# Who issues the loads of the weight ring: POOL or SP

## The chip, the cores and the metric

The kernel runs on one core of a Trainium2 chip. A core has a matrix engine (TensorE, PE in the profile; PEld is its weight load), a vector engine (VectorE, DVE), an engine for activations and copies (ScalarE, ACT), a general one (GpSimd, POOL) and one that mostly issues DMAs (SyncE, SP). Each has its own instruction queue and takes it in order. The metric is the device time of one execution in microseconds, as the median of several runs. Lower is better.

## The reference

Eight batches of sliding-window attention with a distance bias, then a maxout layer:

```python
scores = scale * np.matmul(q, k.transpose(0, 1, 3, 2))        # q, k, v: 8 x 8 heads x 576 x 64
mask = (rel >= 0) & (rel < 128)
scores = np.where(mask, scores + bias[None], -1000000000.0)
...                                                           # softmax over keys
attn_out = np.matmul(attn, v)
x = attn_out.transpose(0, 2, 1, 3).reshape(B * S, H * D)      # 4608 x 512
h = np.maximum(np.maximum(x @ w1, x @ w2), x @ w3)            # w1, w2, w3: 512 x 768
return h @ w_out                                              # w_out: 768 x 512
```

## The kernel before

Attention works on pairs of heads: four tasks per batch, five blocks of 128 queries each. `load` (line 288) and `load_v` (line 293) fetch the inputs of a task through SP into pools of two buffers. `products` (314), `score` (344, 348), `normalise` (367), `turn` (transposes, 376, and mask cuts on POOL, 390 and 394) and `mix` (416) compute it.

The maxout layer of a batch is a sequence of 11 groups: nine of the three weight matrices, cut into columns (`g` below 9), and two of the output matrix (`g` 9 and 10 of the unit's count, which read the resident tiles `ow`). From batch 1 on each group multiplies 2 x 2 blocks with seven products in place of eight, so a group has seven units, a batch 77, and a unit is 6 matmuls (9 for the output matrix) of 128 x 128 by 128 x 288 at line 623. Every operand is held as a high and a low part, and each product takes three matmuls. `factors_x` and `factors_h` build the sums and differences of the blocks; `split` (442 on ACT, 443 on POOL or DVE) makes the high and low parts. `put` takes results out of PSUM: maxima and sums on DVE (544 to 552), copies on ACT (632), and at line 537 the store of an output tile through SP.

The seven factor tiles of a group's weights are computed once, in the first two batches, and kept in DRAM as `keep[g][a]`, in two halves: `a` 0 with four tiles (1024 KB) and `a` 1 with three (768 KB). From batch 2 on they are read back for each batch. This is the weight ring: the pool `wt_p` has `RING = 2` buffers for each half. `stream` is called at the end of each unit and puts the next load into the program, if `ahead` says that the last unit that reads the buffer two groups back has been written down:

```python
def ahead(n, a):
    return (n - RING, 6 if a else 3) in used
```

The units of a group come in the order 0, 1, 6 of the group before, 2, 3, 4, 5. Units 0 to 3 read half 0; units 4, 5 and 6 read half 1. So half 1 comes free two units before half 0 of the next group does, and the loads come in pairs.

All events of the program are sorted by a due time written by hand (`at`), and a tile framework then orders each engine's queue at compile time, places the waits, and lets an instruction that needs a buffer wait until the buffer's last reader is through. From batch 2 on, `pe` keeps the matmuls in the order of the program (`tc.keep_in_program_order`, 277); the other engines' orders are the framework's.

After the last batch's attention (from about 721 us) the rest is the maxout layer alone: this document calls it the tail.

Of the kernel before, what the change touches and what calls it, by code (L numbers as in the profile page):

```python
# [8 lines left out]
F32 = mybir.dt.float32  # L9
# [20 lines left out]
def attention_maxout_kernel(  # L30
# [11 lines left out]
    nc = tc.nc  # L42
# [76 lines left out]
    keep = [[dram.tile([P, e, 2, W], F32, name=f"keep{g}_{a}") for a, e in enumerate((4, 3))] for g in range(9)]  # L119
# [3 lines left out]
    wts = {}  # L123
# [87 lines left out]
    def place(n, a):  # L211
        wts[n, a] = wt_p.tile([P, 4 - a, 2, W], F32R, name=f"wt{a}")

    def ahead(n, a):

        return (n - RING, 6 if a else 3) in used
# [48 lines left out]
    def stream():  # L265
        nonlocal streamed
        n, a = divmod(streamed, 2)
        if n < 9 * B and prepared == STEPS and ahead(n, a):
            place(n, a)
            nc.gpsimd.dma_start(wts[n, a], keep[n % 9][a])  # L270
            streamed += 1

    fixed = False
# [319 lines left out]
    def unit(u):  # L593
# [33 lines left out]
        if g < 9:  # L627
            used.add((at, k))
        stream()
        if k < 3:  # L630
            e = part_of[n, "e", k] = t_p.tile([P, C], F32, name="t")
# [112 lines left out]
```

## Time and profile before

| | |
|---|---|
| median of 3 runs | 817.06 us (815.86 to 818.38) |
| the profiled execution | 818.97 us |
| its span, first to last instruction | 817.3 us |
| mean granted clock of TensorE | 0.970 |
| bytes moved by DMA | 187.96 MB, of which 99.10 MB by the loads that POOL issues |
| busy share of PE, PEld, DVE, ACT, POOL | 93%, 82%, 66%, 65%, 34% |

In a line of a timeline or of the chain, the first number is the start in us from the start of the span and the second the length in us; a bracket at the end gives the idle time of the engine before the instruction and what ended it. A line of waits has the total in us, the number of times and the longest. A line of DMA issues has the count, the size of one in KB and the median time from issue to landing. A line of windows has the stretch, its length, the busy time of PE, PEld, DVE, ACT and POOL with their instruction counts, the granted clock, the busy share of the 16 DMA engines and GB/s. "SPq" and "POOLq" are the queues of the engines that issue DMAs.

### The profile page before, as it was taken

The numbers are of one execution on the slowest core, as the hardware profiler recorded it, in microseconds if no ns is written. First come the engines' busy times: TensorE is split into PE (matmuls) and PEld (weight loads), VectorE is DVE, ScalarE is ACT, GpSimd is POOL, SyncE is SP. The second block draws the span as 40 slices with busy tenths as digits, with TensorE's granted clock in tenths as the row PEclk, the third lists the DMA queues.
The fourth block names the chain that finished last, engine by engine and source line by source line (L and its number), as shares of the span: only waits on it lengthen the run. The fifth ranks groups of instructions, "written<-read, shape, count | busy, mean of one in ns | idle before, by whom it ended". The sixth has DMA issues, their size and how long they took to land.

```text
span 817.3 us, 18140 instructions
## 1 busy us (share of the span) xinstructions
PE 761.5 (93%) x6344; PEld 673.1 (82%) x6344; DVE 538.2 (66%) x1756; ACT 528.7 (65%) x1736; POOL 281.8 (34%) x515
## 2 busy tenths in 40 slices
PE   4767998999889999999999999999999999999987
PEld 1335988898778898899888998899888998899887
DVE  5777878479997756693757756694657746573552
ACT  6988888478776656676667656676667656552332
POOL 1211223111433325542544325542544325531431
PEclk7776999999999999999999999999999999999999
DMA  7875786388888458863887458873787457855851
GB/s 268 279 243 171 246 280 214 111 287 272 289 278 299 138 190 292 285 238 135 263 279 257 165 192 293 281 241 133 268 272 258 163 192 264 253 181 186 303 179 59
DMA packets 53772, 187.96 MB, mean 230 GB/s; under 512 B 5936, under 2 KB 14896, under 8 KB 46768
## 3 DMA queue, kind: packets, MB, share of 16 engines
q0 software_dynamic: 15552, 99.10, 36.6%
q1 hardware_dynamic: 37984, 87.64, 31.5%
q8 instruction: 50, 0.82, 0.4%
q14 instruction: 42, 0.34, 0.1%
q10 hardware_dynamic: 144, 0.07, 0.0%
HBM read 154.53 MB, written 32.24 MB: 229 GB/s over the span
## 4 chain that ended last, share of the span: by engine, by line
PE 61%; DVE 9%; issue 9%; DMA 8%; POOL 6%; ACT 6%; SPq 0%; POOLq 0%; DVEq 0%; ACTq 0%
PE ps_m L623 41%; PE ps_x L416 6%; PE ps_m L585 6%; PE ps_s L314 5%; POOL hs L443 4%; PE pt L376 4%; DMA hs<-w 2%; DMA wt<-keep 2%; DMA hs<-in_w_all 2%; ACT p L348 2%; DMA w<-hs 1%; DVE hs L195 1%; DVE wt L153 1%; ACT p L367 1%; DVE t L549 1%
## 5 line engine op out<-in xcount | busy, mean ns | idle before, releaser
L623 PE MATMUL ps_m<-xs,wt 128*128 128x288 f32 x2646 | 375.4, 298 | 16.5 <-DVE hq L552 8.6
L623 PEld LDWEIGHTS ps_m<-xs,wt 128*128 128x128 f32 x2646 | 356.0, 188 | 24.7 <-DVE hq L552 11.2
L390 POOL TENSOR_SCALAR_AFFINE_SELECT pp<-pr 128x256 f32<-128x256 f32 (+1 forms) x128 | 54.6, 426 | 294.2 <-ACT pr L389 170.4
L348 ACT ACTIVATE p<-s,st 128x128 f32<-128x128 f32 (+1 forms) x320 | 127.2, 401 | 18.1 <-DVE st L344 18.0
L632 ACT COPY t<-ps_m 128x288 f32<-128x288 f32 x231 | 89.4, 392 | 75.3 <-PE ps_m L623 75.3
L623 PE MATMUL ps_m<-hs,ow 128*128 128x288 f32 x882 | 124.5, 298 | 3.0 <-POOL hs L443 1.4
L443 POOL TENSOR_TENSOR hs<-hq,hs 128x288 fp32r<-128x288 f32 x106 | 90.6, 862 | 102.6 <-ACT hs L442 102.4
L623 PEld LDWEIGHTS ps_m<-hs,ow 128*128 128x128 f32 x882 | 118.8, 189 | 5.1 <-POOL hs L443 2.1
L367 ACT ACTIVATE p<-p,st 128x128 f32<-128x128 f32 (+1 forms) x320 | 108.9, 395 | 13.9 <-DVE st L360 13.8
L270 POOL DMA_DIRECT2D wt<-keep x108 | 59.8, 554 | 106.1 <-PE ps_m L623 104.5
L344 DVE CUSTOM_DVE_ANT_0 s<-ps_s,bias 128x128 f32<-128x128 f32 (+1 forms) x300 | 76.7, 281 | 17.8 <-PE ps_s L314 10.9
L416 PE MATMUL ps_x<-pp,v 128*64 128x256 f32 (+3 forms) x768 | 80.8, 338 | 4.7 <-POOL pp L390 4.5
L332 DVE COPY_PREDICATED ps_s<-prev,ps_s 128x256 f32<-128x256 uint8 x120 | 50.8, 423 | 50.1 <-PE ps_s L314 48.7
L549 DVE TENSOR_TENSOR t<-ps_m,t 128x288 f32<-128x288 f32 x126 | 56.3, 452 | 37.4 <-PE ps_m L623 21.5
L314 PE MATMUL ps_s<-qk 64*64 64x192 f32 (+1 forms) x1080 | 69.6, 335 | 9.5 <-DMA qk<-in_qk 4.9
L442 ACT CAST hs<-hq 128x288 fp32r<-128x288 f32 x117 | 48.5, 430 | 39.2 <-DVE hq L550 20.9
L416 PEld LDWEIGHTS ps_x<-pp,v 128*64 128x64 f32 (+1 forms) x768 | 46.1, 142 | 30.8 <-issue 10.1
L376 PE MATMUL pt<-ident,p 128*128 128x128 f32 (+1 forms) x320 | 59.1, 295 | 12.4 <-ACT p L367 8.5
L376 PEld LDWEIGHTS pt<-ident,p 128*128 128x128 f32 (+1 forms) x320 | 34.4, 144 | 41.4 <-issue 18.2
L585 PE MATMUL ps_m<-xs,wt 128*128 128x288 f32 x432 | 63.0, 306 | 3.3 <-DVE xs L443 2.6
L585 PEld LDWEIGHTS ps_m<-xs,wt 128*128 128x128 f32 x432 | 60.5, 196 | 4.3 <-DVE xs L443 3.2
L314 PEld LDWEIGHTS ps_s<-qk 64*64 64x64 f32 x1080 | 41.0, 137 | 26.8 <-issue 10.6
(60 smaller groups left out, 853.0 us busy)
## 6 DMA issues: line engine op xcount, KB each, us to landing
wt<-keep POOLq DMA_DIRECT2D x54, 1024.0 KB, 7.4
wt<-keep POOLq DMA_DIRECT2D x54, 768.0 KB, 4.7
qk<-in_qk SPq DMA_DIRECT2D x31, 576.0 KB, 6.4
hs<-in_w_all SPq DMA_DIRECT2D x24, 512.0 KB, 4.9
v<-in_v SPq DMA_DIRECT2D x32, 320.0 KB, 4.5
keep<-wt SPq DMA_DIRECT2D x36, 256.0 KB, 4.0
outT<-t SPq DMA_DIRECT2D x64, 144.0 KB, 1.8
wt<-keep SPq DMA_DIRECT2D x27, 256.0 KB, 4.5
```

The source lines that it names most:

```text
L270: nc.gpsimd.dma_start(wts[n, a], keep[n % 9][a])
L314: pe(nc.tensor.matmul(ps[j][d:d + D, o:o + k1 - k0], lhsT=qkt[t][j * D:(j + 1) * D, 0, q0:q0 + D], rhs=qkt[t][j * D:(j + 1) * D, 1, k0:k1] ...
L344: nc.vector.tensor_tensor_reduce(out=s[:n], in0=ps[j][:n, P:2 * P], in1=(bias if i else bias0)[:n, 2 * hp + j, :], scale=-0.125, scalar=3. ...
L348: nc.scalar.activation(p[:n, j], s[:n], AF.Exp, bias=st[:n, 0, a, j:j + 1], scale=-1.0, accum_out=st[:n, 1, a, j:j + 1])
L367: nc.scalar.activation(p[:n, j], p[:n, j], AF.Copy, scale=st[:n, 2, a, j:j + 1])
L376: pe(nc.tensor.transpose(out=pt[:, a, j, :n], in_=p[:n, j], identity=ident[:n, :n]))
L416: pe(nc.tensor.matmul(x[j * D:(j + 1) * D, c:c + e - a], lhsT=vv[:n, i, j * D:(j + 1) * D], rhs=w[:n, j].rearrange("p a b -> p (a b)")[:, ...
L443: e.tensor_tensor(out=lo, in0=src, in1=hi.bitcast(F32), op=ALU.subtract)
L549: nc.vector.tensor_tensor(out=s, in0=ps, in1=e, op=ALU.add)
L585: pe(nc.tensor.matmul(ps, lhsT=lt, rhs=rt, start=m == 0 and c == 0, stop=m == len(pairs) - 1, skip_group_check=True,))
L623: pe(nc.tensor.matmul(ps, lhsT=lt, rhs=rt, start=i == 0 and k in (0, 1, 4), stop=i == len(pairs) - 1, skip_group_check=True,))
L632: nc.scalar.copy(out=e, in_=ps)
```

## The change

The load in `stream` is issued by SP (`nc.sync`) in place of POOL (`nc.gpsimd`), and the tile that it fills is named as plain 32-bit floats in the call, as the other loads into these tiles do (line 190). Nothing else is edited.

```diff
@@ -267,7 +267,7 @@
         n, a = divmod(streamed, 2)
         if n < 9 * B and prepared == STEPS and ahead(n, a):
             place(n, a)
-            nc.gpsimd.dma_start(wts[n, a], keep[n % 9][a])
+            nc.sync.dma_start(wts[n, a].bitcast(F32), keep[n % 9][a])
             streamed += 1
```

## The prediction

> **What bounds the kernel now.** I read the page first, then the list of whom TensorE waited for, cut at 740 us, then the chain of waits, and last the timelines of PE, POOL and SP.
>
> ```profile
> span 817.3 us, 18140 instructions
> PE 761.5 (93%) x6344; PEld 673.1 (82%) x6344; DVE 538.2 (66%) x1756; ACT 528.7 (65%) x1736; POOL 281.8 (34%) x515
> ```
>
> PE is busy for 93% of the span; POOL, which the change relieves, for 34%. The first question is therefore where PE waits for something that POOL does. The answer for PE from 260 to 740 us, whole:
>
> ```profile
> PE ps_m L623 <- DVE hq L552: 6.8, 5, 1.4
> PE ps_m L623 <- POOL hs L443: 1.4, 2, 1.1
> PE ps_m L623 <- ACT t L632: 0.2, 1, 0.2
> ```
>
> Columns: total us, times, longest. No wait for a load of the weight ring stands in it. The windows and the chain show the same for one batch:
>
> ```profile
> 494.00:586.00 92.00, 90.46 (x792) 81.63 (x786) 59.11 (x203) 60.03 (x207) 37.49 (x69) 1.00 0.70 234
> 494.99 1.52 POOL hs L443 x2
> ...
> 496.75 0.41 POOL pp L390
> ...
> 497.52 1.54 POOL hs L443 x2
> ...
> 586.98 1.52 POOL hs L443 x2
> ```
>
> The same step of the chain comes back after 586.98 - 494.99 = 92.0 us, so a batch takes 92.0 us, in which PE computes for 90.46. The idle 1.5 us are mostly the one wait of 1.4 us per batch for line 552. Its chain runs through POOL, but through splits (443) and mask cuts (390, and 394 after it), and no load stands in it.
>
> After the last attention step the picture differs. PE between 750 and 800 us, with the idle time before each piece and what ended it:
>
> ```profile
> 756.78 11.60 PE L623 MATMUL ps_m<-xs,wt 128*128 128x288 f32 x84 [0.55 <-DMA wt<-keep]
> 769.44 11.43 PE L623 MATMUL ps_m<-xs,wt 128*128 128x288 f32 x84 [1.05 <-DMA wt<-keep]
> 781.65 5.83 PE L623 MATMUL ps_m<-xs,wt 128*128 128x288 f32 x42 [0.78 <-DMA wt<-keep]
> 788.37 5.83 PE L623 MATMUL ps_m<-xs,wt 128*128 128x288 f32 x42 [0.90 <-DMA wt<-keep]
> ```
>
> Here PE stops four times for the ring, 0.55 + 1.05 + 0.78 + 0.90 = 3.3 us. A group of 42 matmuls takes 5.83 us. A half of the ring is asked for nine units ahead of its use (units of the group before, and two or four more), 9/7 x 5.83 = 7.5 us here, against 9/77 x 92.0 = 10.75 us in a batch with attention.
>
> **The change part by part.** It takes 108 DMA issues from POOL's queue and puts them into SP's; the transfers, their sizes and the matmuls that free the slots stay.
>
> ```profile
> L270 POOL DMA_DIRECT2D wt<-keep x108: 527/553/704, 249.2 to 785.1; - x108
> L190 SPq DMA_DIRECT2D wt<-keep x27: 319/376/1242, 142.8 to 247.7; - x27
> wt<-keep POOLq DMA_DIRECT2D x54, 1024.0 KB, 7.4
> wt<-keep POOLq DMA_DIRECT2D x54, 768.0 KB, 4.7
> qk<-in_qk SPq DMA_DIRECT2D x31, 576.0 KB, 6.4
> v<-in_v SPq DMA_DIRECT2D x32, 320.0 KB, 4.5
> keep<-wt SPq DMA_DIRECT2D x9, 768.0 KB, 4.4
> ```
>
> *Removed from POOL:* 108 x 0.553 = 59.7 us. Up to 740 us I cost that at nothing: the cover is PE's 90.46 of 92.0 us, and the one chain through POOL starts from ACT, not from a load. If POOL were the bound, it would be worth 59.7.
>
> *Added to SP:* 108 x 0.376 = 41 us of issues, spread over the 540 us in which SP mostly stands at a wait. Cost nothing.
>
> *The queues that it is moved past.* On POOL a load stands behind splits. In the tail, with the start, the length and the idle time before it:
>
> ```profile
> 747.74 0.53 POOL L270 DMA_DIRECT2D wt<-keep  x1 [3.43 <-PE ps_m L623]
> 749.34 0.53 POOL L270 DMA_DIRECT2D wt<-keep  x1 [1.07 <-PE ps_m L623]
> 753.34 0.53 POOL L270 DMA_DIRECT2D wt<-keep  x1 [3.47 <-PE ps_m L623]
> ...
> 759.73 0.58 POOL L270 DMA_DIRECT2D wt<-keep  x1 [0.84 <-PE ps_m L623]
> 761.07 0.80 POOL L443 TENSOR_TENSOR hs<-t,hs 128x288 fp32r<-128x288 f32 x1 [0.77 <-ACT hs L442]
> 761.84 2.33 POOL L443 TENSOR_TENSOR hs<-hq,hs 128x288 fp32r<-128x288 f32 x3
> 764.13 0.57 POOL L270 DMA_DIRECT2D wt<-keep  x1
> ...
> 773.97 0.53 POOL L270 DMA_DIRECT2D wt<-keep  x1 [1.07 <-PE ps_m L623]
> ...
> 783.06 0.57 POOL L270 DMA_DIRECT2D wt<-keep  x1
> ```
>
> Where POOL was idle, it issued as soon as PE freed the slot: the second load of a pair 1.60 us after the first (747.74, 749.34), the next pair 4.00 us later (753.34). By that rhythm the load of 764.13 could have gone at 759.73 + 1.60 = 761.33, and it went 2.8 us late, behind four splits. The load of 783.06 could have gone at 773.97 + 4.00 + 1.60 = 779.57, and went 3.5 us late. PE's stops at 769.44 and 788.37 are these two (the chain has each load as the piece ahead of the stop).
>
> *Stop at 769.44:* issued at 761.33 and landing after 7.4 us (the median of the 1024 KB loads, nearest to a load that follows its pair's first one) it is there at 768.73. PE's idle time began at 769.44 - 1.05 = 768.39, so 0.34 us are left.
> *Stop at 788.37:* 779.57 + 7.4 = 786.97, before 787.47, when PE stopped. All 0.90 go.
> *Landing from SP:* 768 KB take 4.4 us from SP (towards DRAM) and 4.7 from POOL, the nearest pair of rows of one size: I take 0.3 us sooner. That leaves 0.04 at 769.44 (1.0 gained), and takes 0.3 from each of the other two stops, whose loads were not late.
>
> Sum: 1.0 + 0.9 + 0.3 + 0.3 = 2.5 us. Bounds: all four stops gone, 3.3 us. On the other side a load might land later from SP: the 576 KB row of SP takes 6.4 us, and 448 KB more at queue 0's rate (99.10 MB in 36.6% of 817.3 us, 331 GB/s) are 1.4, so 7.8 for 1024 KB, 0.4 later than from POOL. Then the stop at 769.44 keeps 0.7, the 0.9 go, and each of the seven pairs of the tail may stop PE for 0.4: 2.8 - 1.2 = 1.6 us lost. I take the 2.5, since the pair of one size is nearer than the scaled one.
>
> ```profile
> q0 software_dynamic: 15552, 99.10, 36.6%
> q1 hardware_dynamic: 37984, 87.64, 31.5%
> ```
>
> Both queues move bytes at about the same rate, 2.7 and 2.8 MB for each per cent, so I expect no change from the engines' side.
>
> *What is late next:* in the tail the transfers. At 765 to 770 us they are nearly full, while in the slice before, where the late load was missing, they had room:
>
> ```profile
> 760.00:765.00 5.00, 5.00 (x38) 4.85 (x37) 2.11 (x5) 2.43 (x7) 3.93 (x6) 1.00 0.74 263
> 765.00:770.00 5.00, 3.94 (x30) 3.74 (x29) 2.57 (x6) 1.13 (x4) 1.86 (x3) 1.00 0.96 324
> ```
>
> *The new wait on SP.* A load waits for its slot, and behind it stand the next qk and v loads and the output stores; and a load can stand behind their waits. SP's queue, in a batch:
>
> ```profile
> 559.56 0.34 SPq L288 DMA_DIRECT2D qk<-in_qk  x1
> 563.57 0.33 SPq L537 DMA_DIRECT2D outT<-t  x1
> 568.15 18.10 SPq L293 DMA_DIRECT2D v<-in_v  x2
> SPq L293 <- PE ps_s L314: 143.4, 9, 17.7
> ```
>
> The last line (SP's waits, 260 to 720 us) says that SP stands for up to 17.7 us at one v load. That costs nothing as long as the queue is sorted by the order in which PE releases things. It looks sorted today: qk, store and v go in the order of their release, though the program writes qk and v in strict turn. The qk, v and ring loads are all freed by PE, whose order line 276 fixes from batch 2 on. So I cost it at nothing.
>
> The profiled execution took 818.97 us, 1.7 around its span, and 1.9 above the median of 817.06. Taken off its time: 816.5; off the median: 814.5.
>
> **The rivals.** *Nothing changes.* The tail would be bound by transfers: 0.96 of the engines' time at 765 to 770 us speaks for it, 0.74 just before against it. Then only the shorter issue is gained, 0.553 - 0.376 = 0.18 us at four stops, 0.7 us: 816.4. The Trainium skill, "DMA: Bandwidth & Descriptors", section "Issuing engines are not separate DMA queues", says that all issuers share the same 16 engines and that another issuer saves only sequencer time. By that rule 816.4 would be the time; the trace agrees on the shared engines, but shows loads 2.8 and 3.5 us late in POOL's queue, which that rule does not price.
>
> *A load behind a v load in SP's queue (slower).* If the fixed order puts one ring load behind a v load that waits, it goes up to 17.7 us late. In a batch the room is 10.75 us less a landing of 6.0 (the median between 260 and 740 us): 4.7 us, from which point it decides. At half the longest wait, 8.9 us, PE stops 4.2 us; once in each of the five batches from 260 to 720 us that is 21 us: 838 (835 with the gain in the tail). Against it: the sorted order above.
>
> ```profile
> DMA to landing us min/median/max: 4.5/6.0/8.6
> ```
>
> *One queue for all.* Two queues share the engines today; in one, a ring load could have to wait for a whole qk load ahead of it: 590 kB at 331 GB/s, 1.8 us, and 8.6 + 1.8 = 10.4 us is still inside 10.75. With a v load ahead as well (320 KB, 1.0 us) it is 11.4, a stop of 0.65 us, for four such meetings in each of five batches 13 us: 830. Against it: a load that shares pays for the other's bytes already, so the 8.6 contains them. The same page, section "Queues, rings and completion order", has each engine take turns between queue rows packet by packet; by that rule the turns are lost with one row, and 830 is what it would come to. No row here shows two big loads in one queue.
>
> *More than predicted.* The compile-time order of POOL and DVE may shift once the loads are off POOL. If the cuts of lines 390 and 394 (497.52 - 496.75 = 0.77 us) fall behind the splits, five stops shrink by 0.77, 3.9 us: 810.6. The same freedom can cost as much: 818.4.
>
> **How the numbers follow.** The measurement tells 0.3%, 2.45 us, from no change: below 814.6 is faster, above 819.5 slower. My forecast lies on that line. Chances: as forecast 0.45 (812.5 to 816.5, a little over half of it under the line); nothing changes 0.24; more than predicted 0.13; a load behind a v load 0.08; one queue for all 0.04; lost by order or by slower landing, up to 1.6 + 3.9 us, 0.06. Faster: 0.27 + 0.13 = 0.40. Slower: 0.08 + 0.04 + 0.04 = 0.16. The rest, 0.44, is the same. The range from 809.5 to 820.5 leaves out the two rivals with long stops and the far ends.
>
> **What would show it.** Right: no issue by line 270 on POOL, 108 more on SP; the splits in the tail follow one another with no load between; the loads of the tail come in pairs 1.6 us apart; PE's wait for the ring falls from 3.3 us to about 0.8; batches stay at 92.0 us. Wrong: PE waits for the ring between 260 and 740 us, or a ring load on SP that is issued right after a v load's long wait; the tail's transfers over 0.9 throughout with the stops unchanged; batches off 92.0 us at equal DMA waits, which would be the order on POOL and DVE.

## The result: slower, though the loads themselves got better

The changed kernel takes 828.29 us (median of 4 runs, 826.73 to 831.05) against 817.26 us before (4 runs, 815.86 to 818.38): a ratio of 1.0131 with a 95% interval of 1.0094 to 1.0168, 11.0 us slower. The profiled execution took 826.73 us, its span 825.0 us, which is 7.7 us longer than the span before.

The page of the changed kernel, first its busy times, then DMA issues (count, KB of one, median us from issue to landing):

```profile
span 825.0 us, 18158 instructions
PE 767.9 (93%) x6344; PEld 677.9 (82%) x6344; DVE 534.2 (65%) x1756; ACT 529.9 (64%) x1736; POOL 224.2 (27%) x407
...
q1 hardware_dynamic: 53536, 186.74, 66.1%
...
wt<-keep SPq DMA_DIRECT2D x54, 1024.0 KB, 6.9
wt<-keep SPq DMA_DIRECT2D x54, 768.0 KB, 4.3
```

POOL has lost 108 instructions and 57.6 us, the ring loads land 0.5 and 0.4 us sooner than from POOL, and nearly all bytes (186.74 of 187.96 MB) go through one hardware queue. PE has the same 6344 matmuls but is busy for 6.4 us more, so part of the loss is not waiting at all.

Whom PE waited for, from 260 us to the end (total us, times, longest):

```profile
PE ps_m L623 <- ACT t L632: 10.0, 10, 2.0
PE ps_m L623 <- DVE hq L552: 3.7, 7, 1.7
PE ps_m L623 <- DVE hq L544: 3.6, 6, 0.6
PE ps_m L623 <- POOL hs L443: 1.4, 2, 1.1
...
```

The two lines left out are one wait each, of 0.8 and 0.6 us, for lines 443 and 535 of DVE. No wait for the ring is left, neither in a batch nor in the tail. Waits for line 632 (a copy by ACT) and line 544 (a maximum by DVE) have come instead. The long ones recur once a batch. PE's timeline of the changed kernel in two batches, with the idle time before each piece in the bracket:

```profile
310.55 1.05 PE L623 MATMUL ps_m<-xs,wt 128*128 128x288 f32 x6 [1.77 <-ACT t L632]
311.80 3.46 PE L623 MATMUL ps_m<-xs,wt 128*128 128x288 f32 x24 [0.20 <-DVE hq L552]
332.04 1.06 PE L623 MATMUL ps_m<-xs,wt 128*128 128x288 f32 x6 [0.63 <-DVE hq L544]
...
404.16 1.06 PE L623 MATMUL ps_m<-xs,wt 128*128 128x288 f32 x6 [1.77 <-ACT t L632]
405.40 4.99 PE L623 MATMUL ps_m<-xs,wt 128*128 128x288 f32 x24 [0.19 <-DVE hq L552]
```

and the windows between one such stop and the next, of the changed kernel and (the last line) of the kernel before at its own stops:

```profile
310.55:404.16 93.61, 90.78 (x785) 81.63 (x785) 59.08 (x203) 60.19 (x207) 27.97 (x52) 1.00 0.66 231
404.16:499.31 95.15, 92.33 (x784) 83.19 (x784) 59.00 (x203) 60.29 (x207) 27.97 (x52) 0.98 0.66 224
499.31:594.61 95.30, 92.30 (x784) 83.14 (x785) 58.43 (x203) 60.29 (x207) 27.91 (x52) 0.98 0.66 227
594.61:689.75 95.14, 92.32 (x785) 83.17 (x785) 59.00 (x203) 60.30 (x207) 28.00 (x52) 0.98 0.65 225
...
405.40:407.50 2.10, 2.10 (x9) 2.10 (x10) 0.80 (x4) 1.38 (x6) 0.00 (x0) 0.52 0.79 331
```

```profile
407.96:499.96 92.00, 90.45 (x785) 81.66 (x785) 59.40 (x203) 60.02 (x207) 37.48 (x69) 1.00 0.70 236
```

A batch takes 93.6 us where the granted clock stays at 1.00, and 95.2 where it doesn't; before it took 92.0. The first step is idle time: 1.77 + 0.20 + 0.63 at these three pieces in place of one stop of 1.34. The second is clock: after the stop at 404 us it is 0.52 for 2.1 us, and 24 matmuls take 4.99 us in place of 3.46. The sum of the four batches is 379.2 us against 368.0, 11.2 lost. The rest, from the last of these stops to the end, is 825.0 - 689.75 = 135.25 us against 817.3 - 683.94 = 133.36 before, 1.9 lost. The stretch ahead of the first stop goes the other way: 310.55 us against 315.97, though no load of line 270 is issued in its first 249 us. So the loss from there on is 13.1 us, and 5.4 won earlier in this execution leave the 7.7 us of the spans. Those 5.4 us are no gain of the change: the first stretch differs from execution to execution, and in experiment 3, which is the kernel before up to its last batch, the same stop ends at 308.29 us.

The tail shows the ring's gain and what ate it. PE of the changed kernel:

```profile
749.54 20.55 PE L623 MATMUL ps_m<-xs,wt 128*128 128x288 f32 x150
771.75 15.62 PE L623 MATMUL ps_m<-xs,wt 128*128 128x288 f32 x114 [1.66 <-DVE hq L552]
787.79 1.86 PE L623 MATMUL ps_m<-xs,wt 128*128 128x288 f32 x12 [0.41 <-DVE hq L544]
790.79 9.46 PE L623 MATMUL ps_m<-xs,wt 128*128 128x288 f32 x69 [1.14 <-DVE hq L552]
```

The four ring stops (3.3 us) are gone, and three stops behind DVE, 1.66 + 0.41 + 1.14 = 3.2 us, stand in their place.

**Where a batch loses it.** DVE's timeline of the changed kernel, just ahead of the stop at 404 us:

```profile
398.94 0.45 DVE L544 TENSOR_TENSOR hq<-ps_m,hq 128x288 f32<-128x288 f32 x1
402.33 0.46 DVE L446 TENSOR_TENSOR hq<-hq,t 128x288 f32<-128x288 f32 x1 [2.95 <-POOL hs L443]
402.71 0.75 DVE L446 TENSOR_TENSOR xt<-xk 128x576 f32<-128x576 f32 x1
403.38 0.41 DVE L332 COPY_PREDICATED ps_s<-prev,ps_s 64x256 f32<-64x256 uint8 x1
```

and of the kernel before, at the same place of its batch:

```profile
402.61 0.76 DVE L446 TENSOR_TENSOR xt<-xk 128x576 f32<-128x576 f32 x1 [0.37 <-ACT xk L425]
403.28 0.41 DVE L332 COPY_PREDICATED ps_s<-prev,ps_s 64x256 f32<-64x256 uint8 x1
...
407.08 0.46 DVE L446 TENSOR_TENSOR hq<-hq,t 128x288 f32<-128x288 f32 x1 [1.34 <-POOL hs L443]
407.45 1.18 DVE L552 TENSOR_TENSOR hq<-ps_m,t 128x288 f32<-128x288 f32 x3
```

The instruction `hq<-hq,t` of line 446 is the subtraction `sub(b10, b10, t)` of `factors_h`, in its branch for block (1, 0). It must not overwrite `b10` before POOL has split it. Before, it stood behind the sum `xt`, the mask of line 332 and the scores. Now it stands ahead of all of them, while the splits are still running. DVE stands 2.95 us for it. On ACT the copy of the next split waits for the subtraction, and the copy of line 632, which frees the PSUM tile that PE wants, stands behind that:

```profile
402.83 0.43 ACT L442 CAST hs<-hq 128x288 fp32r<-128x288 f32 x1 [2.18 <-DVE hq L446]
...
403.69 0.41 ACT L632 COPY t<-ps_m 128x288 f32<-128x288 f32 x1
```

The edit touches no instruction of DVE or ACT. But the framework orders these queues at compile time, and with 108 instructions taken from POOL it wrote other orders of DVE, ACT and POOL (PE's is fixed from batch 2 on and is the same in both). Is it the order that costs, or something that the loads do to it?

### The profile page after: what moved, and what is told of

The parts are those of the page before. It is cut to its first block, busy times and chain, and to the rows that moved or that the text cites. A ratio compares the mean times of both kernels' runs of the same rounds, so it can differ in the third digit from the quotient of the medians.

```text
span 825.0 us, 18158 instructions
## 1 busy us (share of the span) xinstructions
PE 767.9 (93%) x6344; PEld 677.9 (82%) x6344; DVE 534.2 (65%) x1756; ACT 529.9 (64%) x1736; POOL 224.2 (27%) x407
## 2 busy tenths in 40 slices
DMA packets 53772, 187.96 MB, mean 228 GB/s; under 512 B 5936, under 2 KB 14896, under 8 KB 46768
## 3 DMA queue, kind: packets, MB, share of 16 engines
q1 hardware_dynamic: 53536, 186.74, 66.1%
## 4 chain that ended last, share of the span: by engine, by line
PE 54%; DVE 16%; ACT 10%; issue 8%; POOL 8%; DMA 3%; SPq 0%; POOLq 0%; ACTq 0%; DVEq 0%
PE ps_m L623 35%; POOL hs L443 6%; PE ps_m L585 6%; PE ps_x L416 5%; PE ps_s L314 4%; PE pt L376 3%; ACT p L348 3%; DVE t L446 2%; DVE xs L443 2%; DVE t L549 2%; DVE hq L550 2%; DMA hs<-in_w_all 1%; ACT p L367 1%; DVE s L344 1%; ACT hs L442 1%
## 5 line engine op out<-in xcount | busy, mean ns | idle before, releaser
L623 PE MATMUL ps_m<-xs,wt 128*128 128x288 f32 x2646 | 382.0, 301 | 19.9 <-ACT t L632 10.1
L623 PEld LDWEIGHTS ps_m<-xs,wt 128*128 128x128 f32 x2646 | 361.9, 191 | 28.7 <-ACT t L632 12.6
L348 ACT ACTIVATE p<-s,st 128x128 f32<-128x128 f32 (+1 forms) x320 | 127.0, 400 | 18.3 <-DVE st L344 17.9
L367 ACT ACTIVATE p<-p,st 128x128 f32<-128x128 f32 (+1 forms) x320 | 109.0, 396 | 13.8 <-DVE st L360 12.6
L376 PEld LDWEIGHTS pt<-ident,p 128*128 128x128 f32 (+1 forms) x320 | 34.2, 143 | 40.3 <-issue 17.7
L585 PE MATMUL ps_m<-xs,wt 128*128 128x288 f32 x432 | 62.4, 303 | 3.5 <-DVE xs L443 2.6
L585 PEld LDWEIGHTS ps_m<-xs,wt 128*128 128x128 f32 x432 | 59.5, 193 | 4.7 <-DVE xs L443 3.1
L550 DVE TENSOR_TENSOR hq<-t,hq 128x288 f32<-128x288 f32 x126 | 61.2, 490 | 2.3
L348 ACT ACTIVATION_READ_ACCUMULATOR p<-s,st 128x1 f32 (+1 forms) x320 | 61.6, 193 | 0.0
```

What stands on the lines that cost most here:

```text
L348: nc.scalar.activation(p[:n, j], s[:n], AF.Exp, bias=st[:n, 0, a, j:j + 1], scale=-1.0, accum_out=st[:n, 1, a, j:j + 1])
L367: nc.scalar.activation(p[:n, j], p[:n, j], AF.Copy, scale=st[:n, 2, a, j:j + 1])
L376: pe(nc.tensor.transpose(out=pt[:, a, j, :n], in_=p[:n, j], identity=ident[:n, :n]))
L550: nc.vector.tensor_tensor(out=h, in0=s, in1=h, op=ALU.max)
L585: pe(nc.tensor.matmul(ps, lhsT=lt, rhs=rt, start=m == 0 and c == 0, stop=m == len(pairs) - 1, skip_group_check=True,))
L623: pe(nc.tensor.matmul(ps, lhsT=lt, rhs=rt, start=i == 0 and k in (0, 1, 4), stop=i == len(pairs) - 1, skip_group_check=True,))
```

## The experiments

Two theories. *Order:* the loads from SP help, and the new order of DVE, ACT and POOL costs more than they bring. *Loads:* the loads from SP, in one queue with the others, disturb the rest, and the order is innocent. An order is pinned by edges between neighbours of one engine's queue, which add no wait on the chip, at the end of the function that the change touches:

```diff
+    traced = {i.name: i for i in nc.cur_bb.bb.instructions}
+    link = mybir.DependencyInfo(mybir.DependencyClass.NoSync, mybir.DependencyReason.DATA)
+    for seq in ORDER.values():
+        names = [n for n in (f"I-{k}" for k in seq) if n in traced]
+        for x, y in zip(names, names[1:]):
+            tc.add_manual_dep(traced[y], x, link, reason="order")
```

`ORDER`, a list of instruction numbers for each pinned queue, differs from kernel to kernel and is described with each. Ratios below are to the kernel before, run beside each kernel (its medians: 817.18 us in the first four, 817.43 in the last four).

**1. The loads by SP, in the order of before.** The change, and `ORDER` with the queues of DVE, ACT and POOL as they were built before the change.

> Loads from SP as in the changed kernel, but DVE, ACT and POOL take their compute instructions in the very order of the kernel before (edges at compile time, no new waits). Theory (the order did it): batches of 92.0 us again, one stop of PE per batch of about 1.4 us behind line 552, no stop for the ring in the tail: 813 to 816 us. Rival (the loads in SP's queue do it themselves, by their transfers or their waits): 825 to 831 us, batches of about 93.5 us.

Measured: 813.48 us (809.35 to 820.84), ratio 0.9962 (0.9932 to 0.9993). Its waits of PE from 260 us on, and PE in the tail:

```profile
PE ps_m L623 <- DVE hq L552: 6.8, 5, 1.4
...
PE ps_m L623 <- DMA wt<-keep: 1.4, 3, 0.9
```

```profile
755.46 11.43 PE L623 MATMUL ps_m<-xs,wt 128*128 128x288 f32 x84 [0.15 <-DMA wt<-keep]
767.16 17.37 PE L623 MATMUL ps_m<-xs,wt 128*128 128x288 f32 x126 [0.27 <-DMA wt<-keep]
785.46 5.83 PE L623 MATMUL ps_m<-xs,wt 128*128 128x288 f32 x42 [0.94 <-DMA wt<-keep]
```

The same loads, from the same queue, and the kernel is faster than before instead of slower. Line 552 is where it was, and the ring stops fall from 3.3 us to 1.4, where none was expected. The theory of the loads has fallen.

The stop of 0.94 us that is left is the one that took 0.90 before. Its load in the chain of this run, and (the last line) in the chain of the kernel before:

```profile
777.30 8.02 DMA wt<-keep
...
783.06 5.17 DMA wt<-keep
```

From SP it goes out 0.02 us after PE has freed the slot, but it takes 8.02 us to land in place of 5.17. The 16 DMA engines are busy for 0.88 to 0.98 of each 5 us from 755 to 785 us here, so what is left of the ring stops goes with full transfers and no longer with a late issue.

**2. The loads by POOL, in the order of after.** The kernel before, and `ORDER` with the queues of the changed kernel.

> The converse: loads from POOL as before, but DVE, ACT and POOL take their compute instructions in the order of the changed kernel. Theory (the order did it): stops of PE of 1.8 us behind line 632 and 0.6 us behind line 544 in each batch, batches of 93.5 to 95 us, 826 to 833 us, with POOL's delayed loads still in the tail. Rival (the loads in SP's queue): 817 us as before.

Measured: 835.83 us (832.88 to 838.05), ratio 1.0239 (1.0208 to 1.0271). Its waits of PE:

```profile
PE ps_m L623 <- ACT t L632: 9.1, 5, 2.0
PE ps_m L623 <- DVE hq L544: 8.1, 5, 1.6
```

The stops come with the order and without the change. The time is a little over the 826 to 833 us that were expected. The stop behind line 544 is 1.6 us in place of 0.63 here: the issue of a load (0.57 us at 331.68) stands between POOL's splits, and DVE's subtraction just ahead of line 544 takes 2.04 us in place of 0.45. In this order too the loads are better off on SP: 828.29 against 835.83, 7.5 us.

**3. Only the last batch's 18 loads by SP.**

```diff
-            nc.gpsimd.dma_start(wts[n, a], keep[n % 9][a])
+            nc.sync.dma_start(wts[n, a].bitcast(F32), keep[n % 9][a]) if n >= 9 * B - 9 else nc.gpsimd.dma_start(wts[n, a], keep[n % 9][a])
```

> Only the 18 loads of the last batch are issued by SP, the other 90 by POOL; the order of the engines changes from there on only. Theory: batches stay at 92.0 us, the four stops for the ring (3.3 us) go, some new stops for DVE come in the tail as in the changed kernel (about 3 us there): 815 to 818 us. Rival (each load in SP's queue costs its share of 11 us): 18 of 108, about 819 us.

Measured: 814.77 us (812.56 to 818.71), ratio 0.9988 (0.9966 to 1.0009), which can't be told from no change. The ring wait fell as wanted, but the total wait for line 552 grew:

```profile
PE ps_m L623 <- DVE hq L552: 8.9, 7, 1.4
...
PE ps_m L623 <- DMA wt<-keep: 0.7, 2, 0.5
```

Two of the seven waits are new ones in the tail, of 1.36 and 0.83 us, which the kernel before doesn't have; the other five are its own 6.8 us. So 18 loads off POOL were enough for new stops behind DVE, at the place where the loads went.

**4. The loads by SP, DVE alone in the order of before.** The change, and `ORDER` with one list. ACT's and POOL's queues are left to the framework.

> Loads from SP, DVE alone in the order of the kernel before, ACT and POOL free. If the order of DVE carries the loss: 813 to 817 us. If the order of ACT or POOL carries it: up to 828 us. Rival (the loads in SP's queue themselves): 825 to 831 us.

Measured: 815.4 us (813.9 to 818.34), ratio 0.9983 (0.9961 to 1.0005). Of the 11 us lost all come back with DVE's queue, and the stops behind line 632 go. The stops of 0.6 us behind line 544 stay (3.2 us in all), so those belong to ACT's or POOL's order. In the tail 3.0 us of ring stops are left here, 2.0 of them in one.

**5. One instruction.** The change, and five edges alone: in each of batches 2 to 6 the subtraction behind the third maximum of line 552.

```diff
+ORDER = {"4424":[4404,4424],"5771":[5751,5771],"7118":[7098,7118],"8465":[8445,8465],"9810":[9790,9810]}
```

> The changed kernel with five edges of order alone: in each of the batches 2 to 6 (counted from 0) the subtraction of line 446 that waits for POOL's splits goes behind the third maximum of line 552 on DVE; all else is left to the framework. Theory (this one subtraction, taken too early, blocks DVE for 2.9 us): the stop of 1.8 us behind line 632 goes in every batch, and the low clock that follows it; 826.7 - 5 x (1.8 + up to 1.3) gives 811 to 819 us. Rival (the order of the other instructions carries it): 825 us or more.

Measured: 815.53 us (813.61 to 817.45), ratio 0.9972 (0.995 to 0.9994). PE's waits:

```profile
PE ps_m L623 <- DVE hq L552: 3.5, 7, 1.7
PE ps_m L623 <- DVE hq L544: 3.2, 5, 0.6
...
PE ps_m L623 <- ACT t L632: 1.2, 5, 0.2
```

Moving one instruction per batch takes 12.8 us off the 828.29. In the built queues nothing else changed its place but the split that reads the subtraction's result (line 442 on ACT, 443 on POOL), which moves back with it. The wait for line 632 falls from 10.0 to 1.2 us, and the clock of the trace stays up at the places where it fell.

**6. The same instruction the other way.** Experiment 4, but with DVE's list changed so that the five subtractions stand as early as in the changed kernel.

> Loads from SP and DVE in the order of the kernel before, as in the run that gave 815.4 us, but with the five subtractions of line 446 put early, ahead of the scores of the step, as in the changed kernel. Theory (this one subtraction): the stop of 1.8 us behind line 632 is back in each batch, with or without the low clock: 819 to 827 us. Rival (the other moves on DVE): 815 us.

Measured: 836.1 us (832.01 to 837.08), ratio 1.0206 (1.0176 to 1.0237), 20.7 us more than experiment 4. The sign was expected, the size wasn't. Its waits, a piece of PE, and the window that begins there:

```profile
PE ps_m L623 <- DVE hq L552: 17.9, 5, 3.6
```

```profile
412.29 4.97 PE L623 MATMUL ps_m<-xs,wt 128*128 128x288 f32 x24 [3.62 <-DVE hq L552]
...
412.30:417.30 5.00, 5.00 (x28) 4.84 (x32) 0.66 (x2) 1.75 (x6) 0.00 (x0) 0.66 0.13 52
```

The stop stands at line 552 and not at 632, and it is 3.6 us, since DVE stands 3.70 us for the subtraction in this list and all three maxima of line 552 follow behind the sums of lines 357 and 360 (the changed kernel has the first maximum ahead of both). 17.9 less the 8.1 of experiment 4 is 9.8 us of idle time. The other half, some 2 us a batch, goes with the clock: in every batch the window behind the stop shows 0.50 to 0.67.

**7. The best of both.** The loads by SP, the orders of before, and in them the five subtractions behind the three maxima of line 552.

> Loads from SP, all engines in the order of the kernel before, except that the five subtractions go behind the maxima of line 552 on DVE. Theory: PE's stop of 1.36 us per batch behind line 552 shrinks, since DVE no longer waits for POOL's splits ahead of it: 813.5 - 5 x 1.0 to 1.36 gives 806 to 809 us. If the maxima wait as long for something else: 813 us.

Measured: 804.82 us (804.0 to 806.81), ratio 0.9837 (0.9815 to 0.9859), the fastest of all and a little under the 806 to 809 us that were expected. No stop behind line 552 is left from 260 us on; what remains of the ring waits is in the tail:

```profile
PE ps_m L623 <- DMA wt<-keep: 1.8, 3, 1.1
```

**8. Is that the order alone?** The kernel before, loads by POOL, with the five edges of experiment 5.

> The kernel before, loads from POOL, with the same five edges. Theory: the stop behind line 552 shrinks as well, 817.2 - 5 x 1.0 to 1.36 gives 810 to 812.5 us, and the ring's four stops of the tail, 3.3 us, stay. Then the loads in SP's queue are worth 2 to 4 us beside it. If the loads on POOL hold the gain up: 817 us.

Measured: 814.41 us (812.36 to 816.06), ratio 0.9948 (0.9928 to 0.9968). That is over the 810 to 812.5 us that were expected. The wait for line 552 is gone here too, but PE now waits for the ring instead, two of the six times in a batch with attention (1.38 and 1.40 us):

```profile
PE ps_m L623 <- DMA wt<-keep: 7.4, 6, 2.1
```

In 7 the subtraction's place and the issuing engine together give 12.6 us. Alone they give 3.0 (8) and 3.7 us (1): with the stop at line 552 gone, PE waits for the loads from POOL 7.4 us, and for those from SP 1.8 us. Apart from the loads, the built queues of 7 and 8 differ in one copy of line 632 per batch, by one place on ACT.

What wasn't tried: why the framework places the subtraction early when POOL is freed. That the built orders differ is shown, and that the difference costs the time is shown; the rule by which it chose is open.

## Why the prediction was wrong

- *The loads: right in sign and sum, not in each term.* The issues are SP's, the tail's splits have no load between them, and the ring waits fell. With the order held (experiment 1) the kernel takes 813.48 us where 814.5 was forecast, and the ring wait left was 1.4 us where about 0.8 was forecast. But "All 0.90 go" failed: that stop is still 0.94 us, and its load took 8.02 us to land where 7.4 was taken. The stop at 781.65 made up for it, 0.78 us gained where 0.3 was forecast. So the nearness of the sum is in part luck. The landings came 0.5 and 0.4 us sooner in the changed kernel, where 0.3 was assumed, but that is not general: in experiment 7 the medians from SP are 7.2 and 5.3 us, against 7.4 and 4.7 from POOL.
- *SP's queue at no cost: right.* Neither "a load behind a v load" nor "one queue for all" happened: PE has no wait for the ring in the changed kernel. SP's waits over the whole span, first the load's own wait for a slot and then the v loads':

```profile
SPq L270 <- PE ps_m L623: 310.1, 107, 7.7
SPq L293 <- PE ps_x L416: 36.8, 15, 4.7
```

  The v loads' waits did not hold the ring up; the longest of a v load is 4.7 us, where the second rival reckoned with up to 17.7.
- *"Nothing changes": wrong for most of the stops.* Transfers did not bind all of the tail before: the ring stops fell from 3.3 to 1.4 us with the order held. (In the changed kernel they all went, but there three stops behind DVE gave the loads more time.) They bind what is left, as "what is late next" said.
- *POOL's 59.7 us costed at nothing: the step that failed.* The working asked what POOL's own time was worth, and found it covered. It is covered. But with the loads off POOL the orders of DVE, ACT and POOL changed, and the sum took them as given. The prediction did name this, as "more than predicted" with its reverse ("the same freedom can cost as much: 818.4"), and priced it at two mask cuts of POOL, 0.77 us a batch, with a chance of 0.06 for a loss by order or slower landing. These cuts did fall behind the splits (404.08 us in the changed kernel, where the splits that the subtraction waits for end at 402.30; before, they stood between those splits at 404.76). But a subtraction on DVE moved as well, and that is what cost: 1.6 us a batch of idle time and small slowing, and another 1.5 us in three of five batches by the clock; with the tail's three new stops 13.1 us in the trace against 3.9.
- *What would have shown it beforehand.* The row was in the profile of before: `hq<-hq,t` waits for POOL's splits (1.34 us of idle DVE at 407.08), and the one stop of PE per batch hangs on it. An instruction that makes its whole engine wait is worth a price for "and if it stands earlier": the place that it got, ahead of `xt`, is at 402.61 in that trace, 4.5 us before 407.08, with POOL's splits still to be waited for, and `xt`, the scores, line 552 and ACT's copies behind it.
- *The sign to look for* was named: "batches off 92.0 us at equal DMA waits, which would be the order on POOL and DVE". That is what the trace showed, with the DMA waits even smaller.

## What to carry to other kernels

Where a framework orders the queues at compile time, moving an instruction off one engine edits the program of all the others: compare the built orders before the times, and judge the move with the order held. The loads on SP gained 3.7 us in the old order, 7.5 in the new one and 9.6 in the best one, and seemed to cost 11 since another order came with them. And look for the instruction on an in-order queue that waits longest for another engine: here the place of one 0.46 us subtraction per batch was worth 3.0 us (8 against the kernel before), 8.7 (7 against 1), 12.8 (5 against the changed kernel) or 20.7 (6 against 4).

## What the runs showed of the hardware

The granted clock can fall after short stops. In the changed kernel it fell to 0.52 behind a stop of 1.77 us and one of 0.19 us (405.40), and did not fall behind the same two stops in another batch (311.80). In experiment 1 it fell once, behind a single stop of 1.35 us:

```profile
405.86 3.46 PE L623 MATMUL ps_m<-xs,wt 128*128 128x288 f32 x24 [1.35 <-DVE hq L552]
...
497.74 4.97 PE L623 MATMUL ps_m<-xs,wt 128*128 128x288 f32 x24 [1.35 <-DVE hq L552]
```

The same stop costs 1.5 us more the second time (4.97 - 3.46). Behind 3.6 us (experiment 6) it fell in every batch. In experiment 4 it fell behind none of five stops of 1.51 to 1.65 us:

```profile
679.94 3.45 PE L623 MATMUL ps_m<-xs,wt 128*128 128x288 f32 x24 [1.64 <-DVE hq L552]
```

So a stop of PE is not worth its length alone: here 1.8 us of idle time cost up to 3.3.

The low stretches of the changed kernel from 260 us on have one length. The clock is 0.50 in these two windows and in a third, 596.61 to 600.02, and it is 1.00 in the 3.41 us before and after the first:

```profile
405.47:408.88 3.41, 3.41 (x14) 3.41 (x15) 0.73 (x3) 1.64 (x6) 0.00 (x0) 0.50 0.50 211
501.04:504.45 3.41, 3.41 (x17) 3.41 (x16) 0.32 (x1) 1.49 (x4) 0.00 (x0) 0.50 0.42 178
```

From one start to the next it is 95.57 us, 28 times 3.413, though the stops ahead of them are 95.15 and 95.30 us apart: the clock changes on steps of its own. Half of the clock for 3.41 us is 1.7 us, which is about what the matmuls lose (1.5).

The Trainium skill, "TensorE: Matmul & The Clock Gate", part 1 on the clock gate, has the clock go down after an idle window of about 3.4 us, and says that the window runs freely. The stop of 3.6 us agrees; those of 1.35 and 1.77 us are shorter than that and lowered it all the same, so the measurement differs from the page. The steps of 3.41 us above agree with a window of that length that runs freely. What a step must hold for the clock to fall stays open: 1.35 us was enough once in experiment 1, and 1.64 was not in experiment 4.
